# Local and downsampled attention with two expert layers: the first layer's input scale taken from v, its first two inputs split in two halves

## The chip, the cores and the metric

One core of a Trainium2 chip runs the whole program. The metric is the device time of one execution in microseconds (us), as the median of several runs. TensorE (PE) multiplies matrices, VectorE (DVE) and ScalarE (ACT) work on elements, GpSimd (POOL) helps them, and SyncE's queue (SP) issues all DMA transfers.

## What is computed

Attention over q, k, v of shape (4 batches, 8 heads, 576 tokens, 64), as the sum of a downsampled part and a part limited to a band, then two dense layers with a gate:

```python
out_d = sm_attn(q_d, k_d, v_d)              # q, k, v averaged over 4 tokens
out_up = np.repeat(out_d, factor, axis=2)
mask = np.abs(pos[:, None] - pos[None, :]) < factor
scores = np.where(mask, scale * q @ k.T, -1e9)
out_local = softmax(scores) @ v
x = (out_up + out_local)                    # to 2304 tokens x 512
h = x @ w_in;  g = h / (1 + exp(-h));        x = g @ w_out     # layer 1, 512 -> 2048 -> 512
h = x @ w_in2; g = h / (1 + exp(-1.702 * h)); out = g @ w_out2 # layer 2
```

The weights are stored as 64-bit floats. Both softmax rows are positive and sum to at most 1, so every element of x is at most twice the largest |v| of its batch.

## The kernel before

Work goes in blocks of half a batch: 8 blocks m of 288 tokens in layer 1, 9 blocks of 256 tokens in layer 2. A block of attention has four units u = 4m + hp, one for each pair hp of heads. The program is a list of named steps, each for one engine. Every engine takes its steps in the order of a table (`PLACES`, two digits for each step); tables `ON` give the engine of steps that may run on several. Before an instruction an engine waits for the semaphores of what the step depends on, and what stands behind it on that engine waits too.

**Matrix products.** Each f32 operand is held as two f16 halves, high and low, and a product is three matmuls (`TERMS`). So x must be scaled by a power of two and split: `split` makes the steps `xh` (ACT, the high half, tile xhl, L781) and `xl` (DVE, the low half, L784).

**The scale before.** When x of a unit is ready (step `XA`, DVE L1324 and L1325, tile xf), step `XM` takes the largest |x| of each partition (L1328). When all four are there, `rm` (PE, L769, two passes) sums them over the partitions by a product with ones, `am` (L773) takes the largest of four, and `pw` (three instructions in `pow2`, L286 to L288) makes the power of two and its inverse. Then `xh`, `xl`, and the first product `h1.m.0.0` (PE, L709, 12 matmuls).

**The weights at the start.** Eight loads of 1 MB for the first layer's inner weights (`ldst1in.c.j`, SP L524) and eight for the outer ones. Each is turned from 64 bits to 32 by `ca` and `cz` (ACT, L326 and L330), `cs` (DVE, L334), `sg` (ACT L347 or DVE L339) and `cp` (two half adds on DVE or POOL, L351), its scale is taken (`sps` on PE L563, `si` on DVE), and it is split by `hi` (ACT L379) and `lo` (DVE L383, tile win).

**The attention of block 0** runs beside this. For a unit: `KT` and `QT` transpose k and q on PE (tiles kps L1133, qps L1197), `KC` and `QC` copy them on ACT (QC at L1201), `SC` makes the scores (PE L1221 and L1228), `DM`, `LC`, `LS`, `LE`, `LU`, `RC`, `LN`, `DN` and `PT` are the softmax, `AV` is the product with v (PE L1310), `UC` copies a part out (ACT L1316), and `XA` makes x. Tile vw holds v's rows for the local part: all rows of a pair of heads of the batch, 768 elements in each partition.

**The loads.** The end of the kernel has a list `first` of the first loads (for each pair of heads k, q, v and a weight), but its pairs are soft: a table may put a load elsewhere. q has two buffers, so the third load of q waits until `QT0` has read the first.

Of the kernel before, what the change touches and what calls it, by code (L numbers as in the profile page):

```python
# [8 lines left out]
F32 = mybir.dt.float32  # L9
# [30 lines left out]
def on(name, usual):  # L40
# [8 lines left out]
    "0206040307050k0h0L0V00090n111u010a080J0q0U0Y180f0H0S0N0W0X1o1s0e0w0B0F0Q101C1I0K1r1v1y1z1B1R1V0T1Z1L262g2i2r2x1q2d2n2h2G2o2L2R1S2N2Z2Q"  # L49
    "3k2S3p3u1Q2y2C2O2U2W3R3X171c1e1l1O221F1P1T20252c2u2w2P2Y3x3I353a3Z4l44662m323h3c4q3L3S4w4L2K3o3H4h4r4u4H4X5Q3w4n5b4R5o5d5l5t5I3B4O505c"  # L50
    "5R5K5O616e4C5G5Z5Y64696i6v7f4z5s6a5C6C6r6I6K6Y5r6W6P7a7g7j7z7p7x65797L7i7R7n7r7W824J536f6q6z6F6b6o6H6U70766S747m7C7A7J7O7S7Y8586889u0d"
    "0i0t0O0b0c0j0o0m0v0p0r0y0z0C0A0D0M0I0R0Z12140l0u1j1p0g0s0x0E0G0P13161a1d1g1f1h1m1k1t1D1H1J191i1Y29151b1n1w1x1G1A1E1M1N281X242b2a2e2k2p"
    "2D1K232s2I1U21272j2f2v2l2t2z2A2E2B2F2H2J2M2T2V2X303334393g3b363f3C5a737e8w1W2q374t313e3i3n3q3r3s3v3y3A3E3D3J3W4042484b4D383j3z3M3G3Q3N"
    "3U41454K4f4o4y4M4Q4V4Z514e4m4p4B4v4E4G4N4W565f585g5j5q5v5B5E5M5254595i5e5m5k5p5w5A5F5D5J5L5P5S5X6062686n6D7I7P8Gci3l3t6h4k3d4i6J55678x"
    "7G6x4F8Q7N5V3Y46495n5y636j6g6p6k6G6O6Q6T757b7k6Z7K7U839z3P3T8n5T6c6t726M7E8a8d8f8h8k8l8o8r8u8B8H8L9w7v7Z8K7o7u898j8p8t8C8J8O8P8T8V9197"
    "9b9f9k9m9o8A8I9g8m8s8R928X958Z93989a9d9c9p9v9h9A9G9J9K9Pa1a7a9aqa8cd7t908U9H8E9i9L9R9T9V9Wa4aaacaeafaraxanaBaHaJb79E9Ua2adavataDaGaKaM"
# [1488 lines left out]
```

## Time and profile before

| | |
|---|---|
| median of 3 runs | 883.58 us (882.74 to 883.6) |
| the profiled execution | 883.47 us |
| its span, first to last instruction | 881.7 us |
| PE busy | 858.1 us, 97% of the span |
| DVE busy | 606.1 us, 69% |
| ACT busy | 465.1 us, 53% |
| POOL busy | 151.2 us, 17% |
| mean granted clock of TensorE | 0.986 |

The profile is of one execution. Busy time of PE is modelled for matmuls that overlap, so work on PE is counted below by starts of its instructions. A stretch is given in us from the span's start.

### The profile page before, as it was taken

The page shows a single profiled execution, that of the slowest core. Times are in us where ns is not written, and L with a number is a line of the kernel's source. Part 1 is how long each engine was busy: PE and PEld are TensorE (multiplying, and loading weights), DVE is VectorE, ACT ScalarE, POOL GpSimd, SP SyncE. Part 2 cuts the span into 40 slices and gives each one's busy share as a digit, 9 for nine tenths or more (in the row PEclk, how much of TensorE's full clock was granted, in tenths as well). Part 3 has the DMA queues.
Part 4 walks back from the last instruction along what each step waited for, and adds up shares of the span by engine and source line. Part 5 has one row for each costly group of instructions (what it writes and reads, how often), then busy time and mean ns, then how long its engine had stood idle before and what let it go on. Part 6 is the DMA issues. An engine that isn't in the chain of part 4 may idle for free.

```text
span 881.7 us, 23835 instructions
## 1 busy us (share of the span) xinstructions
PE 858.1 (97%) x10212; PEld 715.9 (81%) x10212; DVE 606.1 (69%) x1342; ACT 465.1 (53%) x824; POOL 151.2 (17%) x186
## 2 busy tenths in 40 slices
PE   6889899999999999999999999999999999999998
PEld 5777677777777777777787788888888888888887
DVE  3889999878876767576576899374474828465472
ACT  4899875645556545574643755253342525253341
POOL 1355333113212321211210011002100000020000
PEclk9869999999999999999999999999999999999999
DMA  9968666266636354533317200000000000000000
GB/s 243 288 181 244 137 116 113 45 130 147 140 66 165 105 124 94 149 94 94 121 31 280 97 1 1 25 1 1 26 26 13 13 13 2 36 2 25 1 15 35
DMA packets 114990, 75.86 MB, mean 86 GB/s; under 512 B 94788, under 2 KB 100292, under 8 KB 113860
## 3 DMA queue, kind: packets, MB, share of 16 engines
q1 hardware_dynamic: 114884, 74.34, 32.3%
q8 instruction: 80, 1.31, 0.7%
q14 instruction: 26, 0.21, 0.1%
HBM read 61.21 MB, written 13.11 MB: 84 GB/s over the span
## 4 chain that ended last, share of the span: by engine, by line
PE 85%; DVE 8%; ACT 4%; DMA 1%; issue 1%; SPq 0%; DVEq 0%; ACTq 0%
PE hps L876 20%; PE hps L709 19%; PE ops L814 19%; PE oy L955 10%; PE oz L955 5%; PE ox L955 2%; PE ul L1310 2%; PE sl L1228 2%; PE sl L1221 1%; PE ul L1304 1%; PE ops L842 1%; ACT st L326 1%; DVE wout L383 1%; DVE g L904 1%; PE tps L1287 1%
## 5 line engine op out<-in xcount | busy, mean ns | idle before, releaser
L709 PE MATMUL hps<-xhl,win 128*128 128x288 f16 x1536 | 199.3, 289 | 0.4 <-DVE tg L724 0.4
L876 PE MATMUL hps<-xhl,win 128*128 128x256 f16 x1728 | 190.3, 273 | 0.0
L876 PEld LDWEIGHTS <-win 128*128 128x128 f16 x1728 | 169.1, 98 | 19.6
L709 PEld LDWEIGHTS <-win 128*128 128x128 f16 x1536 | 148.7, 99 | 38.7 <-issue 0.5
L814 PE MATMUL ops<-g,wout 128*128 128x288 f16 x1344 | 170.9, 286 | 0.0
L955 PEld LDWEIGHTS <-g 128*128 128x128 f16 x1512 | 147.7, 98 | 19.5 <-DVE g L904 1.3
L814 PEld LDWEIGHTS <-wout 128*128 128x128 f16 x1344 | 129.8, 98 | 32.7 <-issue 0.6
L888 ACT ACTIVATE tg<-hps,blk 128x512 f32<-128x512 f32 x72 | 49.4, 687 | 127.6 <-PE hps L876 118.2
L891 DVE SCALAR_TENSOR_TENSOR tg<-tg,hps 128x512 f32<-128x512 f32 x72 | 49.2, 683 | 59.9 <-ACT tg L888 59.9
L904 DVE SCALAR_TENSOR_TENSOR g<-tg,g 128x896 f16<-128x896 f32 x72 | 77.4, 1086 | 0.6 <-ACT g L901 0.3
L955 PE MATMUL oy<-wout,g 128*128 128x256 f16 x648 | 75.1, 273 | 0.0
L901 ACT ACTIVATE g<-tg 128x896 f16<-128x896 f32 x72 | 67.4, 944 | 14.6 <-DVE tg L897 10.4
L721 ACT ACTIVATE tg<-hps,blk 128x576 f32<-128x576 f32 x64 | 47.1, 736 | 43.5 <-PE hps L709 35.7
L351 POOL TENSOR_TENSOR cs<-cs,cz 128x512 int32<-128x512 int32 x32 | 42.0, 1318 | 154.2 <-DVE cs L334 46.0
L724 DVE SCALAR_TENSOR_TENSOR tg<-tg,hps 128x576 f32<-128x576 f32 x64 | 47.8, 747 | 28.6 <-ACT tg L721 28.4
L895 POOL TENSOR_TENSOR tg<-tg 128x128 f32<-128x128 f32 x14 | 9.7, 691 | 293.6 <-DVE tg L891 264.1
L933 ACT ACTIVATE o<-oy,blk 128x256 f32<-128x256 f32 x27 | 12.7, 472 | 73.6 <-PE oy L955 73.6
L734 DVE SCALAR_TENSOR_TENSOR g<-tg,gs,g 128x576 f16<-128x576 f32 x56 | 46.8, 841 | 6.1 <-ACT g L731 6.0
L731 ACT ACTIVATE g<-tg,gs 128x576 f16<-128x576 f32 x56 | 42.6, 768 | 13.1 <-DVE tg L724 12.5
L326 ACT ACTIVATE st<-st 128x512 f32<-128x512 f32 (+1 forms) x48 | 39.6, 830 | 18.1 <-DMA st<-in_moe_w_out_dram 6.9
L939 DVE SCALAR_TENSOR_TENSOR o<-oy,blk,o 128x256 f32<-128x256 f32 x9 | 4.4, 484 | 59.0 <-PE oy L955 34.6
L351 POOL TENSOR_TENSOR x<-x,z 128x512 int32<-128x512 int32 x26 | 35.6, 1384 | 51.5 <-ACT z L330 20.7
(168 smaller groups left out, 1159.3 us busy)
## 6 DMA issues: line engine op xcount, KB each, us to landing
st<-in_moe_w_in_dram SPq DMA_DIRECT2D x8, 1024.0 KB, 9.9
st<-in_moe_w_out_dram SPq DMA_DIRECT2D x8, 1024.0 KB, 5.7
st<-in_moe_w_in_dram SPq DMA_DIRECT2D x16, 512.0 KB, 4.6
st<-in_moe_w_out_dram SPq DMA_DIRECT2D x16, 512.0 KB, 3.9
vw<-in_v_dram SPq DMA_DIRECT2D x62, 96.0 KB, 4.8
out_dram<-o SPq DMA_DIRECT2D x18, 256.0 KB, 3.3
wdin<-cs SPq DMA_DIRECT2D x16, 256.0 KB, 3.6
r<-wdin SPq DMA_DIRECT2D x4, 1024.0 KB, 4.8
```

Of the source, the lines that this page charges most:

```text
L326: ACT.activation(out=hi.bitcast(F32), in_=hi.bitcast(F32), func=AF.Copy, scale=2.0 ** -112)
L351: eng.tensor_tensor(out=s, in0=s, in1=zget()[:, o], op=ALU.add)
L709: nc.tensor.matmul(o, T[w][:, kc, a, fc * P:(fc + 1) * P], T[xk][:, kc, b, :T_], start=(n == 0), stop=(n == 3 * KC - 1))
L721: ACT.activation(out=T[tg], in_=T[ps][:, :, :T_], func=AF.Tanh, scale=T["a" + bk][:, c:c + 1])
L724: DVE.scalar_tensor_tensor(out=T[tg], in0=T[tg], scalar=1.0, in1=T[ps][:, :, :T_], op0=ALU.add, op1=ALU.mult)
L814: nc.tensor.matmul(o, w[:, j, a, dc * P:(dc + 1) * P], g[:, b, j % 2, :], start=(n == 0), stop=(n == 3 * NF - 1))
L876: nc.tensor.matmul(o, T[w][:, kc, a, fc * P:(fc + 1) * P], T[xk][:, kc, b, :], start=(n == 0), stop=(n == 3 * KC - 1))
L888: ACT.activation(out=four(), in_=T[ps][:, 0, :], func=AF.Tanh, scale=T["a" + bk][:, c:c + 1])
L891: DVE.scalar_tensor_tensor(out=four(), in0=four(), scalar=1.0, in1=T[ps][:, 0, :], op0=ALU.add, op1=ALU.mult)
L901: ACT.activation(out=T[g][:, 0], in_=T[tg], func=AF.Copy, scale=GS2)
L904: DVE.scalar_tensor_tensor(out=T[g][:, 1], in0=T[tg], scalar=GS2, in1=T[g][:, 0], op0=ALU.mult, op1=ALU.subtract)
L955: nc.tensor.matmul(T[bank[acc]], g[:, a, slot, :], w, start=first and p == p0 and i == 0, stop=prod in (2, 3, 4) and p == NF // 2 - 1 and ...
```

## The change

It has four parts. (1) In layer 1 the scale of x comes from v. `VM`, one for each batch and pair of heads, takes the largest |v| of each partition of tile vw (768 elements); `XM` is gone. `dx` takes the largest of the four and puts it on the diagonal of a 128 x 128 tile, `rm` multiplies this by ones (f32, 128 columns), and `am` takes the largest of 128. Both blocks of a batch share the scale (`scale_of`), so `dx`, `rm`, `am`, `pw` and the step that scales the gate run for the even blocks alone. (2) `split` makes x of blocks 0 and 1 in two halves, `xh..a`, `xl..a` for the first two pairs of heads and `xh..b`, `xl..b` for the others; the product `h1.m.0.0` waits for both. (3) The tables `ON` and `PLACES` are new. (4) The pools of layer 1 are released after `VM`, `XA` and `am`, where it was `XM`. The list `first` is the same.

```diff
@@ split
-        bank = ("pa1", "rm" + bk, 4 * n + 3.9) if L.n == 1 else ("pr", "rm" + bk)
+        sk = scale_of(L, n)
+        bank = ("pa1", "rm" + bk, 4 * n + 2.9) if L.n == 1 else ("pr", "rm" + bk)
+
+        def z():
+            DVE.tensor_reduce(out=small(L, n, 7), in_=mget(), axis=AX.X, op=ALU.max)
+            T["dg" + bk] = pools["at"].tile([P, 1, P], F32, tag="dg", name="dg", bufs=1)[:, 0]
+            DVE.tensor_scalar(out=T["dg" + bk], in0=T["ident"], scalar1=small(L, n, 7), scalar2=None, op0=ALU.mult)
 
         def a():
...
-            nc.tensor.matmul(T["rm" + bk][:, :KC], ones32, mget(), start=True, stop=True)
+            if L.n == 1:
+                nc.tensor.matmul(T["rm" + bk][:, :P], ones32, T["dg" + bk], start=True, stop=True)
+            else:
+                nc.tensor.matmul(T["rm" + bk][:, :KC], ones32, mget(), start=True, stop=True)
...
-            pow2(T["am" + bk], 1, 13, T["inv" + bk], T["s" + bk], t)
+            pow2(T["am" + bk], 1, 13 - 8 if L.n == 1 else 13, T["inv" + bk], T["s" + bk], t)
+
+        parts = ((0, 2), (2, KC)) if L.n == 1 and n < 2 else ((0, KC),)
 
-        def hi():
-            T[xk] = pools["xhl" + ln].tile([P, KC, 2, T_], F16, tag="xhl", name="xhl")
-            ACT.activation(out=T[xk][:, :, 0, :], in_=src(), func=AF.Copy, scale=T["s" + bk])
+        def hi(k0, k1):
+            if k0 == 0:
+                T[xk] = pools["xhl" + ln].tile([P, KC, 2, T_], F16, tag="xhl", name="xhl")
+            ACT.activation(out=T[xk][:, k0:k1, 0, :], in_=src()[:, k0:k1], func=AF.Copy, scale=T["s" + sk])
...
@@ unit
-        def xmax():
-            DVE.tensor_reduce(out=small(L1, m, 10 + hp), in_=T[X][:, hp, :], axis=AX.X, op=ALU.max, apply_absolute_value=True)
-
+        if half == 0:
+            def vmax():
+                DVE.tensor_reduce(out=small(L1, m, 10 + hp), in_=T[vw].rearrange("p e d -> p (e d)"), axis=AX.X, op=ALU.max,
+                                  apply_absolute_value=True)
+            add("VM" + nm, "DVE", dve(4 * NBL * D), vmax, r=[vw], w=[("vm", b, hp)])
```

Of the tables the diff shows only other digits, so three places of the program follow as they stand on the engines. A DMA that stands on SP in one row with "x2" is two transfers.

DVE from `XA3` to the last part of x of block 0 (tile xf is x, xhl its split, win the inner weights, wi and ibin their scale, x_80 the weights on their way). Before:

```order
L1324 TENSOR_TENSOR xf<-ul_793,us 128x3x24
L1325 TENSOR_TENSOR xf<-ul_794,us 128x2x3x24
L1328 TENSOR_REDUCE blk<-xf 128x1
L383 SCALAR_TENSOR_TENSOR win_2_825<-x_80,bin_88,win_2_825 128x2x512
L773 TENSOR_REDUCE blk<-rm 128x1
L286 TENSOR_SCALAR blk<-blk 128x1
L287 TENSOR_SCALAR blk<-blk 128x1
L288 RECIPROCAL blk<-blk 128x1
L443 TENSOR_REDUCE wi_101<-sps 128x1
L748 TENSOR_SCALAR blk<-ibin_87,blk 128x1
```

and after nine more instructions for the weights' scale and a conversion comes `xl`, L784. Now:

```order
L285 TENSOR_SCALAR blk<-blk 128x1
L286 TENSOR_SCALAR blk<-blk 128x1
L287 RECIPROCAL blk<-blk 128x1
L350 ISA x_80<-x_80,z 128x1024
L333 TENSOR_SCALAR x_80<-st_617 128x1024
L1350 TENSOR_TENSOR xf<-ul_812,us 128x3x24
L1350 TENSOR_TENSOR xf<-ul_813,us 128x3x24
L1351 TENSOR_TENSOR xf<-ul_814,us 128x2x3x24
L801 SCALAR_TENSOR_TENSOR xhl<-xf,blk,xhl 128x2x288
L382 SCALAR_TENSOR_TENSOR win_2_787<-x_80,bin_88,win_2_787 128x2x512
L801 SCALAR_TENSOR_TENSOR xhl<-xf,blk,xhl 128x2x288
```

The scale (L285 to L287) stands ahead of `XA3`, and between `XA3` and the last part of x are only the first half and one `lo`.

DVE further ahead, where the maxima of v stand (tile pd and sc are the softmax, nm and mx its maxima; dg is the diagonal). Now:

```order
L382 SCALAR_TENSOR_TENSOR win_1_614<-x_80,bin_88,win_1_614 128x2x512
L333 TENSOR_SCALAR x_80<-st_558 128x1024
L1355 TENSOR_REDUCE blk<-vw 128x1
L1262 TENSOR_REDUCE nm<-sl 72x2
L1269 TENSOR_TENSOR sc<-sl,cap 128x192
L1272 TENSOR_REDUCE mx<-sc 128x6
L442 TENSOR_REDUCE wi_101<-sps 128x1
L774 TENSOR_REDUCE blk<-blk 128x1
L776 TENSOR_SCALAR dg<-ident,blk 128x128
L1350 TENSOR_TENSOR xf<-ul_701,us 128x3x24
```

This is the last of four `VM` (L1355) and `dx` (L774, L776), ahead of `XA2`.

SP at the first loads, from v of the first pair of heads on (st is a weight, vw is v). Before:

```order
L1099 DMA vw<-in_v_dram 28x64
L524 DMA st_223<-in_moe_w_in_dram 128x2x1024
L524 DMA st_225<-in_moe_w_in_dram 128x2x1024
L1053 DMA qraw<-in_q_dram 96x3x64 x2
L1053 DMA kraw<-in_k_dram 96x6x64 x2
L1099 DMA vw<-in_v_dram 32x12x64 x4
```

Now:

```order
L1125 DMA vw<-in_v_dram 28x64
L1079 DMA qraw<-in_q_dram 96x3x64 x2
L523 DMA st_253<-in_moe_w_in_dram 128x2x1024
L523 DMA st_255<-in_moe_w_in_dram 128x2x1024
L1079 DMA kraw<-in_k_dram 96x6x64 x2
L1125 DMA vw<-in_v_dram 32x12x64 x4
```

The third load of q moved ahead of the second and third weight. The first two loads changed places as well: k before q, and PE begins with `KT0.0`, then `QT0`.

## Rows read from the trace of the kernel before

**Rows 1.** Stretches: us, then busy us (instructions) by engine, PE clock, DMA.

```profile
31.60:52.90 21.30, 15.45 (x310) 13.77 (x304) 18.38 (x45) 21.27 (x38) 9.88 (x9) 0.79 0.91 256
52.90:59.10 6.20, 6.20 (x82) 5.55 (x81) 5.89 (x19) 6.20 (x9) 1.02 (x1) 0.50 0.46 150
59.10:134.50 75.40, 70.74 (x1146) 54.62 (x1135) 72.55 (x174) 62.38 (x110) 33.87 (x30) 0.97 0.70 165
134.50:881.70 747.20, 742.56 (x8384) 621.54 (x8380) 494.77 (x1063) 357.48 (x637) 99.82 (x116) 1.00 0.24 66
```

**Rows 2.** Timeline, PE up to the first product: start us, us, instruction.

```profile
52.84 1.87 PE L563 MATMUL sps<-x,ones 128*128 128x128 bf16 x16 [0.66 <-DVE x L334]
...
54.89 2.89 PE L1197 MATMUL qps<-four,qraw 96*128 96x120 f32 x12
57.76 0.76 PE L1221 MATMUL sl<-kd,qT 64*72 64x144 f32 x4
...
59.14 2.52 PE L709 MATMUL hps<-xhl,win 128*128 128x288 f16 x12
```

**Rows 3.** Timeline of ACT, the same stretch.

```profile
52.54 0.43 ACT L1316 ACTIVATE us<-ul 128x288 f32<-128x288 f32 x1
...
56.08 1.28 ACT L781 ACTIVATE xhl<-xf,blk 128x1152 f16<-128x1152 f32 x1
57.23 0.48 ACT L1201 COPY qT<-qps 128x360 f32<-128x360 f32 x1
```

**Rows 4.** Timeline of DVE, the same stretch.

```profile
53.01 0.37 DVE L1324 TENSOR_TENSOR xf<-ul,us 128x72 f32<-128x72 f32 x2 [0.22 <-ACT us L1316]
53.29 0.30 DVE L1325 TENSOR_TENSOR xf<-ul,us 128x144 f32<-128x144 f32 x1
...
54.00 1.27 DVE L383 SCALAR_TENSOR_TENSOR win<-x,bin,win 128x1024 f16<-128x1024 f32 x1
55.19 0.15 DVE L773 TENSOR_REDUCE blk<-rm 128x1 f32<-128x4 f32 x1
...
55.76 0.17 DVE L288 RECIPROCAL blk<-blk 128x1 f32<-128x1 f32 x1
...
57.43 1.41 DVE L784 SCALAR_TENSOR_TENSOR xhl<-xf,blk,xhl 128x1152 f16<-128x1152 f32 x1
```

**Rows 5.** Groups by line and shape, DVE, 0 to 140 us: busy us, mean ns.

```profile
L724 DVE SCALAR_TENSOR_TENSOR tg<-tg,hps 128x576 f32<-128x576 f32 x9 | 6.6, 738 | 0.8 <-ACT tg L721 0.7
...
L351 DVE CUSTOM_DVE_ANT_0 x<-x,z 128x1024 uint16<-128x1024 uint16 x6 | 4.7, 787 | 0.0
L339 DVE TENSOR_SCALAR z<-st 128x1024 uint16<-128x1024 uint16 x6 | 4.4, 740 | 0.0
...
L1328 DVE TENSOR_REDUCE blk<-xf 128x1 f32<-128x288 f32 x8 | 3.6, 449 | 0.2
...
L1148 DVE TENSOR_REDUCE kd<-kT 128x144 f32<-128x576 f32 x4 | 2.9, 729 | 0.0
L784 DVE SCALAR_TENSOR_TENSOR xhl<-xf,blk,xhl 128x1152 f16<-128x1152 f32 x2 | 2.8, 1414 | 0.0
```

**Rows 6.** Groups by line and shape, DVE, whole span.

```profile
L1480 DVE TENSOR_REDUCE blk<-x 128x4 f32<-128x1024 f32 x9 | 10.9, 1211 | 0.0
```

**Rows 7.** Groups by line and shape, PE, whole span.

```profile
L769 PE MATMUL rm<-blk,ones 128*128 128x4 f32 x34 | 5.6, 234 | 0.0
...
L427 PE MATMUL sp<-dg,ones 128*128 128x128 f32 x8 | 1.5, 274 | 0.0
```

**Rows 8.** Timeline of SP's queue, 9 to 12 us.

```profile
9.62 0.91 SPq L524 DMA_DIRECT2D st<-in_moe_w_in_dram  x2
10.72 0.85 SPq L1053 DMA_DIRECT2D qraw<-in_q_dram  x2
```

**Rows 9.** Timeline of PE, its first two steps.

```profile
6.80 1.61 PE L1197 MATMUL qps<-four,qraw 96*128 96x120 f32 x6 [6.80 <-DMA qraw<-in_q_dram]
8.40 2.89 PE L1133 MATMUL kps<-four,kraw 96*128 96x120 f32 x12
```

More of the change, by code (lines that the diff above doesn't have):

```diff
@@ L720, in tanh @@
             T[tg] = pools["tg" + ln].tile([P, 2, T_], F32, tag="tg", name="tg")
-            ACT.activation(out=T[tg], in_=T[ps][:, :, :T_], func=AF.Tanh, scale=T["a" + bk][:, c:c + 1])
+            ACT.activation(out=T[tg], in_=T[ps][:, :, :T_], func=AF.Tanh, scale=T["a" + sk][:, c:c + 1])
         def g0():
@@ L741, in h_pair, with scale_of @@
         plan.users[g].append(plan.steps[-1])
+    def scale_of(L, n):
+        return f"{L.n}.{n - n % 2 if L.n == 1 else n}"
     def a_scale(L, n, cs):
@@ L785, in lo @@
+        parts = ((0, 2), (2, KC)) if L.n == 1 and n < 2 else ((0, KC),)
[3 more added lines that the diff above has]
+            ACT.activation(out=T[xk][:, k0:k1, 0, :], in_=src()[:, k0:k1], func=AF.Copy, scale=T["s" + sk])
+        def lo(k0, k1):
+            DVE.scalar_tensor_tensor(out=T[xk][:, k0:k1, 1, :], in0=src()[:, k0:k1], scalar=T["s" + sk], in1=T[xk][:, k0:k1, 0, :],
                                      op0=ALU.mult, op1=ALU.subtract)
@@ L787, in split @@
         sc2 = ["scope2"] if L.n == 2 else []
-        add("rm" + bk, "PE", 0.2, a, r=mkey + sc2, w=["rm" + bk], alloc=[bank])
-        add("am" + bk, "DVE", 0.16, b, r=["rm" + bk], w=["am" + bk])
-        add("pw" + bk, "DVE", 0.5, d, r=["am" + bk], w=[("inv", bk)])
-        add("xh" + bk, "ACT", act(KC * T_, 1), hi, r=skeys + [("inv", bk)] + sc2, w=[(xk, "h"), xk], alloc=[("xhl" + ln, xk)])
-        add("xl" + bk, "DVE", dve(KC * T_), lo, r=skeys + [("inv", bk), (xk, "h"), xk], w=[(xk, "l")], lock=True)
+        if L.n == 1 and n % 2 == 0:
+            add("dx" + bk, "DVE", 0.45, z, r=mkey, w=["dg" + bk], alloc=[("dg", "dg" + bk)])
+            mkey = ["dg" + bk]
@@ new lines, in split @@
+        if L.n == 2 or n % 2 == 0:
+            add("rm" + bk, "PE", 0.2, a, r=mkey + sc2, w=["rm" + bk], alloc=[bank])
+            add("am" + bk, "DVE", 0.16 if L.n == 2 else 0.28, b, r=["rm" + bk], w=["am" + bk])
+            add("pw" + bk, "DVE", 0.5, d, r=["am" + bk], w=[("inv", bk)])
+        for k0, k1 in parts:
+            e = "" if k1 == KC else "0"
+            tag = bk + ("" if len(parts) == 1 else "ab"[k0 > 0])
+            x = skeys if L.n == 2 else skeys[k0:k1]
+            add("xh" + tag, "ACT", act((k1 - k0) * T_, 1), lambda k0=k0, k1=k1: hi(k0, k1), r=x + [("inv", sk)] + sc2 + ([xk] if k0 else []),
+                w=[(xk, "h" + e)] + ([] if k0 else [xk]), alloc=[] if k0 else [("xhl" + ln, xk)])
+            add("xl" + tag, "DVE", dve((k1 - k0) * T_), lambda k0=k0, k1=k1: lo(k0, k1), r=x + [("inv", sk), (xk, "h" + e), xk], w=[(xk, "l" + e)], lock=True)
@@ L1359, in unit @@
         uses_x.setdefault(m, []).append(s)
-        add(f"XM{u}", "DVE", dve(HALF), xmax, r=[(X, hp)], w=[(X, hp, "m")])
-        plan.users[X].append(plan.steps[-1])
-        plan.steps[-1].keys.add(X)
     uses_x = {}
@@ L1407 @@
         split(L1, m, lambda m=m: T[f"xf{m}"], [(f"xf{m}", hp) for hp in range(NHP)],
-              [(f"xf{m}", hp, "m") for hp in range(NHP)], lambda m=m: small(L1, m, 10, KC), HALF, None)
+              [("vm", m // 2, hp) for hp in range(NHP)], lambda m=m: small(L1, m, 10, KC), HALF, None)
         for s in plan.steps[i0:]:
-            if s.name[:2] in ("xh", "xl", "rm"):
+            if s.name[:2] in ("xh", "xl"):
                 plan.users[f"xf{m}"].append(s)
@@ L1415 @@
                 a_scale(L1, m, [c])
-        else:
+        elif half == 0:
             a_scale(L1, m, list(range(NC)))
@@ L1455, in scope2 @@
         pools["xhl2"] = es2.enter_context(tc.tile_pool(name="xhl2", bufs=2, reuse_waits="tile"))
-    att = [s for s in plan.steps if s.name[:2] in ("XM", "wd", "as", "LN", "so", "si", "pw") or s.name.startswith("xl1")]
+    att = [s for s in plan.steps if s.name[:2] in ("VM", "XA", "am", "wd", "as", "LN", "so", "si", "pw") or s.name.startswith("xl1")]
     add("scope2", "NONE", 0.0, scope2, w=["scope2"], after=att)
```

93 lines of the change are left out of this document (46 added, 47 removed), and 21 rows, old and new, of the table ON.

## The prediction

> **What bounds the kernel now.** I read the page first: PE is busy for 97% of the span, so the question is where the rest lies. The busy times by stretch answer it [rows 1]. From 134.5 us to the end PE is busy for 742.56 of 747.2 us: nothing that feeds it matters there unless it runs dry, and DVE has 252 us to spare. From 59.1 to 134.5 us two engines are nearly full at once, DVE with 72.55 and PE with 70.74 of 75.4 us: DVE still converts weights and makes the gate's halves, PE does the first block's products. Ahead of that, from 31.6 to 52.9 us, ACT is full (21.27 of 21.3), DVE has 2.9 us left, and PE is not the bound. So the time can move in two ways: the first product at 59.14 us may start sooner, and DVE may be sooner with its list up to 134.5 us. Then I read the timelines of three engines from `UC3` (ACT, 52.54) to this product [rows 2 to 4], and the groups by line for prices [rows 5 to 7].
>
> The reader is to see a tail of 6.60 us between `UC3` and the first product. DVE makes `XA3` from 53.01 to 53.59, then the maximum of x, one `lo`, the scale from 55.19 to 55.93, seven small steps and a conversion, and ends `xl` at about 58.76 [rows 4]. ACT can start `xh` only at 56.08 [rows 3]. [...]
>
> **The sum, part by part.**
>
> The tail. With the scale ready before `XA3`, I lay the new order out by the old prices, from the start of `UC3`. `XA3` ends at +1.05 (53.59). ACT makes the first half of `xh` behind `UC3`, a weight step of 1.05, and the second half: half of 1152 elements is 576, on DVE 0.738 against 1.414 for the whole [rows 5], so a half is 0.74; on ACT I take half of 1.28 and the same 0.06 more, 0.70. The second half ends near +2.9. DVE goes on from +1.05 with 0.74, a `lo` of 1.2 (1.27 less overlap) and 0.74 and has all of x at +3.7, where it was +6.22: **2.5 us sooner**. PE transposes q from +1.05, 2.87 us at the lower clock, and makes scores for 1.38: the first product at +5.3, where it was +6.60: 1.3 us sooner. It is PE, not x, that would then be last.
>
> What is put in front of the tail. Ahead of `XA3` DVE gets four `VM`. No row has 768 elements; 576 take 0.729 and 1024 take 1.211 [rows 5, 6], which bound one, and I take 0.93 on the line between them: 3.7. `dx` is two short instructions, at most the 0.449 of a 288-element maximum each [rows 5] and at least nothing; I take 0.4. `am` and `pw` move here, 0.74 [rows 4], 0.1 more for the longer `am`. Three `XM` of 0.449 leave: -1.35. By the tables two more `sg` of 0.65 (0.740 less overlap) and one more `cp` of about 0.65 (0.787 with two double ones among six) stand here [rows 5]: 1.9. Together **5.4 us more work** ahead of `XA3`. About 2.2 of it stands in the first 31.6 us, where DVE waits for transfers and PE for more than half of the time, and I cost that part at nothing; if this cover were gone it would be 2.2. The other 3.2 meet the 2.9 us that DVE has idle from 31.6 to 52.9 [rows 1]. If they fill every gap, `XA3` slips by 0.3; if they fill none, by 3.2. The gaps are many and short and a maximum of v waits only for a load, so it fills well: I take **1.0 us later**, near the lower end.
>
> The first loads. The load of q for unit 2 now stands ahead of two weights on SP, and it waits for `QT0`, which stands behind `KT0.0`. Before, the weights went out at 9.62 and q at 10.72 [rows 8]. With k first, `KT0.0` takes 2.7 and `QT0` 1.6 from 6.80 on [rows 9]: q goes out at 11.1 and the weights at 12.0, 2.4 us later. Behind them wait every later load of SP and, on ACT and DVE, the conversions. Lower bound nothing, since the DMA engines are at work on what was issued before; upper bound 2.4 for all that follows. The scores of unit 0 come no later than before, and by 31 us ACT has the same amount of steps behind it in both orders, so I take 0 and keep 2.4 for the range.
>
> From the tail to 134.5 us. The same steps remain for DVE: 142 from `xl` to the first gate of block 1 before, 139 now. `XM4` to `XM7` are gone (4 x 0.449), block 1's own `am` and `pw` too (0.74), and three `VM` of batch 1 moved in (2.8) with two halves (0.06): even. As DVE is the fuller of the two, the end of this stretch follows DVE: 2.5 less 1.0 is **1.5 us sooner**. PE has 4.7 us idle there and takes this up.
>
> PE's own work. `rm` is two matmuls, and 8 of layer 1 become 4. By starts a pair cost about 0.25 at full clock, and a pair with 128 columns is near it (means of 234 and 274 [rows 7]). Three of the four that are saved stand after 134.5 us: **0.6 us less**, by busy time at most 1.4, at least nothing.
>
> After 134.5 us DVE loses and gains the same (per batch 8 x 0.449 against 4 x 0.93), beside 252 idle us; a new table may bring PE a wait or take one away. PE has 4.6 us idle in that stretch, part of it at its very end; I take 0, between a gain of 1 and a loss of 3.
>
> Sum: -1.5 - 0.6 = -2.1 from the profiled 883.47: 881.4. The median of the runs is 0.11 above the profiled run, which changes nothing here: **881.4 us**.
>
> [...] In the rows two halves of 576 cost 2 x 0.738 where the whole is 1.414, so a cut costs 0.06 us on DVE [rows 5]. [...]
>
> **The rivals.**
>
> (A) The forecast: the tail shortens and DVE carries v's maxima in its gaps.
>
> (B) DVE has no room. `XA3` slips by 2.5, in the upper part of 0.3 to 3.2, and eats the tail: -2.5 + 2.5 - 0.6 gives 882.9. For it: DVE is busy for 18.38 of 21.3 us already. Against it: all but one of the `VM` may run long before they are needed.
>
> (C) Slower: the load of q blocks SP. Weights 2.4 us late, and `XA3` late by this and by the 3.2 that then find no gap, since DVE waits for weights in order: -2.5 + 2.4 + 3.2 - 0.6 is +2.5, 886.0. It decides from a slip of `XA3` of 4.9 us on (2.5 + 0.6 + 1.8). For it: a `cs` of the delayed weight stands on DVE ahead of unit 1's scores. Against it: transfers overlap.
>
> (D) A larger gain: PE also loses waits in 59.1 to 134.5, where it idles for 4.7 us, because DVE's list is better placed: 3 us more, 878.4.
>
> That the change does not do what it says: the product waits for both halves, so the halves only let two engines overlap; but the order on DVE shows the scale ahead of `XA3`, so the tail must change. No chance of its own.
>
> **How the numbers follow.** A measurement of this kernel can tell about 0.2%, 1.8 us: faster is below 881.8, slower above 885.4. A has 0.42, of which 0.27 lie below 881.8 and 0.15 above; B has 0.22, with 0.20 within 0.2% and 0.02 slower; C has 0.21, slower; D has 0.15, faster. Faster 0.42, same 0.35, slower 0.23. The range reaches from D's place, 878, to 1 us beyond C's, 887, and leaves out some 0.2, where a new table does worse or better than any of these.
>
> **What would show it.** Right: the first product at 57 to 59 us, `XA3` at 53.5 to 55, all of x about 2.6 us behind it; DVE at 95% or more from 20 us on; the end of the dense stretch 1 to 3 us sooner. Wrong: `XA3` after 57 us (B or C); ACT or DVE waiting for a weight's transfer between 15 and 25 us (C); PE idle by more than 6 us after 134.5, which would be a cause that I cost at nothing.

## The result, and the profile after

The changed kernel is slower: 889.12 us median of 4 runs (886.41 to 890.47) against 883.59 beside it, ratio 1.0064 with a 95% interval of 1.0040 to 1.0087. Run again unedited it gave 889.39 (886.61 to 891.43), ratio 1.0068 (1.0049 to 1.0087). The forecast of 881.4 had the wrong sign, and the time lies above the range.

The loss arises before 140 us. Two profiles of the changed kernel, one of 886.41 us and one of 891.43, called the quick and the slow one below, show how it is spread. The first product of block 0 starts at 61.91 and 64.22 us (59.14 before), that of block 1 at 138.0 and 142.2 (134.5 before); from there to the end it is 746.6 and 747.5 us (747.2 before). For the quick one this sums to 2.8 + 0.7 - 0.6 = 2.9 us, the difference of the spans (884.6 and 881.7); for the slow one to 5.1 + 2.6 + 0.3 = 8.0.

The busy times by stretch of the quick profile (us, then PE, weight loads, DVE, ACT, POOL with instructions, PE's clock, DMA share, GB/s):

```profile
31.60:57.60 26.00, 18.06 (x352) 16.05 (x326) 24.64 (x54) 22.38 (x40) 15.00 (x10) 0.74 0.92 260
57.60:61.90 4.30, 4.25 (x72) 3.61 (x71) 4.11 (x8) 4.30 (x7) 1.14 (x1) 0.60 0.94 249
61.90:138.00 76.10, 70.47 (x1139) 53.89 (x1132) 74.41 (x173) 61.95 (x114) 34.37 (x29) 0.98 0.61 153
138.00:884.60 746.60, 742.14 (x8382) 621.30 (x8374) 493.41 (x1038) 357.62 (x639) 107.77 (x117) 1.00 0.24 65
```

Beside [rows 1]: up to `XA3` it is DVE that is now full (24.64 of 26.0 us, where it was 18.38 of 21.3), and ACT has idle time. The last stretch is as it was.

The tail itself does what the change says. DVE of the quick profile (start, duration), which answers to [rows 4]:

```profile
57.71 0.37 DVE L1350 TENSOR_TENSOR xf<-ul,us 128x72 f32<-128x72 f32 x2
58.00 0.30 DVE L1351 TENSOR_TENSOR xf<-ul,us 128x144 f32<-128x144 f32 x1
58.38 0.98 DVE L801 SCALAR_TENSOR_TENSOR xhl<-xf,blk,xhl 128x576 f16<-128x576 f32 x1
59.28 1.27 DVE L382 SCALAR_TENSOR_TENSOR win<-x,bin,win 128x1024 f16<-128x1024 f32 x1
60.47 0.81 DVE L801 SCALAR_TENSOR_TENSOR xhl<-xf,blk,xhl 128x576 f16<-128x576 f32 x1
```

From the start of `XA3` to all of x it is 3.57 us (57.71 to 61.28), before 5.83. But `XA3` starts 4.7 us later. PE of the same profile, as [rows 2]:

```profile
58.11 2.50 PE L1223 MATMUL qps<-four,qraw 96*128 96x120 f32 x12
60.54 0.76 PE L1247 MATMUL sl<-kd,qT 64*72 64x144 f32 x4
61.23 0.76 PE L1254 MATMUL sl<-kT,qT 64*32 64x32 f32 x48
61.91 3.06 PE L709 MATMUL hps<-xhl,win 128*128 128x288 f16 x12
```

Where do 4.7 us come from? First the sum over all that stands ahead of `XA3`, before and in the quick profile, with the two groups of DVE that grew by their length (residues `lo`, then bit steps `cs`; busy us, mean ns):

```profile
0.00:53.01 53.01, 38.67 (x619) 34.32 (x619) 32.94 (x90) 39.12 (x71) 16.55 (x40) 0.88 1.02 256
L383 DVE SCALAR_TENSOR_TENSOR win<-x,bin,win 128x1024 f16<-128x1024 f32 x4 | 5.7, 1456 | 0.6 <-ACT win L379 0.6
L334 DVE TENSOR_SCALAR x<-st 128x1024 int32<-128x1024 int32 x8 | 5.7, 727 | 0.6 <-ACT st L326 0.6
```

```profile
0.00:57.71 57.71, 40.53 (x627) 36.34 (x628) 39.78 (x99) 39.06 (x71) 21.30 (x41) 0.85 0.95 253
L382 DVE SCALAR_TENSOR_TENSOR win<-x,bin,win 128x1024 f16<-128x1024 f32 x4 | 6.9, 1743 | 0.1
L333 DVE TENSOR_SCALAR x<-st 128x1024 int32<-128x1024 int32 x8 | 7.3, 921 | 0.9 <-ACT st L325 0.9
```

DVE is busy for 6.8 us more (39.78 for 32.94) and idle for 2.1 less (17.93 for 20.07): the difference is the slip. Of the 6.8, some 2.7 are the same twelve residues and bit steps, only longer. In time, `UC2` (ACT) starts at 46.81, 1.3 later than before (45.55). Unit 3 then takes 10.5 us to `UC3` at 57.30, before 7.0 (52.54). DVE and PE of the quick profile there:

```profile
43.07 3.48 DVE L382 SCALAR_TENSOR_TENSOR win<-x,bin,win 128x1024 f16<-128x1024 f32 x2
46.48 1.75 DVE L333 TENSOR_SCALAR x<-st 128x1024 int32<-128x1024 int32 x1
48.15 0.94 DVE L1355 TENSOR_REDUCE blk<-vw 128x1 f32<-128x768 f32 x1
49.01 0.44 DVE L1262 TENSOR_REDUCE nm<-sl 72x2 f32<-72x288 f32 x1
```

```profile
45.08 0.71 PE L1336 MATMUL ul<-PT,vw 32*64 32x24 f32 x48
48.28 1.01 PE L562 MATMUL sps<-x,ones 128*128 128x128 bf16 x8 [2.49 <-DVE x L333]
51.03 0.79 PE L781 MATMUL rm<-dg,ones 128*128 128x128 f32 x2 [1.74 <-DVE xf L1350]
51.62 2.77 PE L1198 MATMUL vps<-vw,vsum 128*72 128x128 f32 x12
```

Unit 3's scores were ready at 44.5 us (`SC3` on PE), and DVE took them at 49.01, behind two residues, a bit step and the last maximum of v. PE waited for the bit step, then for x of unit 2 ahead of `rm`, and v's transposes stood behind. POOL's additions ran beside DVE's first two rows (43.31, 4.37 us for two), and these took longer than alone: 3.48 for two of 1.27, 1.75 for one of 0.68.

### The profile page after: what moved, and what is told of

Its sections match the earlier page's. It is cut to its first block, busy times and chain, and to the rows that moved or that the text cites. A ratio compares the mean times of both kernels' runs of the same rounds, so it can differ in the third digit from the quotient of the medians.

```text
span 884.6 us, 23807 instructions
## 1 busy us (share of the span) xinstructions
PE 857.3 (97%) x10204; PEld 715.1 (81%) x10204; DVE 611.7 (69%) x1315; ACT 462.8 (52%) x828; POOL 164.5 (19%) x187
## 4 chain that ended last, share of the span: by engine, by line
PE 86%; DVE 7%; DMA 2%; SPq 1%; ACT 1%; issue 1%; POOL 1%; DVEq 0%; ACTq 0%
PE hps L709 20%; PE hps L902 20%; PE ops L840 19%; PE oy L981 11%; PE oz L981 5%; PE ox L981 3%; PE ul L1336 2%; DMA vw<-in_v_dram 2%; PE sl L1254 2%; DVE wout L382 1%; PE ops L868 1%; PE sl L1247 1%; PE ul L1330 1%; PE tps L1313 1%; DMA kraw<-in_k_dram 1%
## 5 line engine op out<-in xcount | busy, mean ns | idle before, releaser
L721 ACT ACTIVATE tg<-hps,blk 128x576 f32<-128x576 f32 x64 | 47.1, 737 | 24.7 <-PE hps L709 21.3
L350 POOL TENSOR_TENSOR x<-x,z 128x512 int32<-128x512 int32 x25 | 39.9, 1610 | 27.0 <-ACT z L346 9.3
```

Source lines behind the costliest of these rows:

```text
L350: eng.tensor_tensor(out=s, in0=s, in1=zget()[:, o], op=ALU.add)
L721: ACT.activation(out=T[tg], in_=T[ps][:, :, :T_], func=AF.Tanh, scale=T["a" + sk][:, c:c + 1])
```

## The experiments

Theories at the start: more work on DVE (maxima of v, diagonal); the new table (order, engines); the first loads; and, once seen, a toss (which of two engines starts first) that makes the runs differ. Step names are those of the text above; `lk`, `lqqraw`, `vw` are the loads of k, q, v. Each time is a median of 4 to 12 runs, beside 9 to 23 of the kernel before (882.7 to 883.3). Where only places move, the diff shows the order on an engine.

**1. The changed kernel again.** No edit.

> The changed kernel once more, unedited. Its five-run times lay between 886.4 and 890.5 us while the kernel before stays within 1 us. Theory 'noise of one chip': this time it stays within 1 us, near 886 to 889. Theory 'its order sits on an edge' (some transfer or wait that falls one way or the other): it spreads over 3 us or more again, and the spans differ by as much. The profile should again show XA3 near 57.7 us and the first product of block 0 near 61.9, against 53.0 and 59.1 before.

889.39 (886.61 to 891.43): it spreads over 5 us again. The profile taken was of the longest run; on DVE it is the same as the quick one to 0.02 us up to 24.2 us. POOL and DVE of the quick profile, then of the slow one:

```profile
24.76 1.82 POOL L350 TENSOR_TENSOR x<-x,z 128x512 int32<-128x512 int32 x1 [6.91 <-ACT st L325]
```

```profile
24.76 0.69 DVE L333 TENSOR_SCALAR x<-st 128x1024 int32<-128x1024 int32 x1 [0.21 <-ACT st L325]
```

```profile
24.69 1.27 POOL L350 TENSOR_TENSOR x<-x,z 128x512 int32<-128x512 int32 x1 [6.83 <-PE sps L562]
```

```profile
24.77 1.75 DVE L333 TENSOR_SCALAR x<-st 128x1024 int32<-128x1024 int32 x1 [0.22 <-ACT st L325]
```

In the slow profile POOL starts 0.08 us ahead of DVE, keeps its own length, and DVE takes 1.06 us longer; in the quick one both start at 24.76, DVE keeps its 0.69 us, and POOL takes 0.55 us longer. In the slow profile, where DVE lost, PE waited for its result, and what followed on PE ran at a granted clock of 0.50 (27 to 31 us):

```profile
26.57 1.01 PE L562 MATMUL sps<-x,ones 128*128 128x128 bf16 x8 [0.77 <-DVE x L333]
27.38 1.57 PE L1223 MATMUL qps<-four,qraw 96*128 96x120 f32 x6
28.75 2.77 PE L1159 MATMUL kps<-four,kraw 96*128 96x120 f32 x12
```

Those 12 transposes take 1.50 us in the quick profile. The stretches say the same, quick first:

```profile
27.00:31.00 4.00, 4.00 (x36) 3.71 (x34) 3.90 (x10) 3.27 (x6) 0.30 (x1) 0.90 1.08 372
```

```profile
27.00:31.00 4.00, 4.00 (x23) 4.00 (x21) 3.83 (x13) 1.84 (x3) 0.51 (x1) 0.50 1.06 386
```

From 34 us on every ACT step of the slow profile is 2.7 to 3.0 us behind the quick one: 1.1 from the toss, the rest from the clock. That the lost toss brings the low clock is not shown: in the profiles of the kernels 2, 9, 10 and 17 DVE loses the same toss, and the granted clock is 1.00 from 24 to 34 us. Kernel 10, its PE wait (1.26 us, longer than the 0.77) and its stretch:

```profile
26.25 0.62 PE L562 MATMUL sps<-x,ones 128*128 128x128 bf16 x8 [1.26 <-DVE x L333]
24.00:34.00 10.00, 7.54 (x166) 6.59 (x166) 9.62 (x23) 8.69 (x14) 3.77 (x3) 1.00 1.15 275
```

Those four are no faster in the median (888.36, 889.70, 888.63 and 891.64).

**2. The first steps as before.**

```diff
 SP
-lk0.0 lqqraw0 lk0.1 lqqraw1 vw0.0 lqqraw2 ldst1in.0.2 ldst1in.1.0
+lqqraw0 lk0.0 lqqraw1 lk0.1 vw0.0 ldst1in.0.2 ldst1in.1.0 lqqraw2
 ACT
-KC0.0 QC0 DE0 LE0 ca1.in.0.0 KC0.1 QC1 cz1.in.0.0
+cz1.in.0.0 ca1.in.0.0 QC0 KC0.0 DE0 LE0 QC1 KC0.1
 PE
-KT0.0 QT0
+QT0 KT0.0
```

> The changed kernel, with only the first steps put back: q ahead of k in the first two loads, q of unit 2 behind two more weights on SP, the first weight's two ACT conversions at the head of ACT, q's transposes ahead of k's. Theory 'first loads': the weights go out 3 us sooner (near 9.7 us in place of 12.7), ACT starts near 6 in place of 10.5 us, and XA3 comes 2 to 4 us sooner, near 54 to 56; time 3 us less than the changed kernel's, 884 to 886. Theories 'more work on DVE' and 'order of unit 3': XA3 moves by under 1 us and the time by under 1 us.

888.36, ratio 1.0057 (1.0041 to 1.0073), 0.8 to 1.0 less than the changed kernel and within its interval. The weights do go out 3 us sooner, SP of the changed kernel and of this one:

```profile
12.69 0.97 SPq L523 DMA_DIRECT2D st<-in_moe_w_in_dram  x2
```

```profile
9.68 0.91 SPq L523 DMA_DIRECT2D st<-in_moe_w_in_dram  x2
```

but `XA3` starts at 57.07, only 0.6 sooner: the load was covered, and this theory falls.

**3. Small maxima of v.** Of v's 768 elements 64 are looked at; the rest of the maximum is left out.

```diff
-in_=T[vw].rearrange("p e d -> p (e d)"), axis=AX.X, op=ALU.max,
+in_=T[vw][:, 1, :], axis=AX.X, op=ALU.max,
```

> The changed kernel, with each maximum of v taken over 64 of its 768 elements (the rest of v's maximum is left out, all else is kept). 0.91 to 0.94 us of DVE a piece become some 0.2, so about 2.9 us of DVE work ahead of XA3 go and 5.8 up to the end of the stretch. Theory 'more work on DVE': XA3 and the first product come 2.5 to 3 us sooner, time 3 to 4 us less. Theory 'first loads' or 'order of unit 3': DVE only waits longer, XA3 moves by under 1 us, time by under 1.5 us.

887.44, ratio 1.0049 (1.0031 to 1.0066): 1.7 to 1.9 less for 2.9 us of work ahead of `XA3` (197 ns each in place of some 930), but the interval overlaps that of the unedited kernel. In its profile, of the longest run (889.73), `XA3` starts at 60.17, where the slow profile of the unedited kernel has 60.53: seen there, smaller maxima bring next to nothing.

**4 to 8. Repairs of the order**, each made to the changed kernel.

```diff
 4 PE
-sps1.in.1.0 QT2
+QT2 sps1.in.1.0
 5 ON
-cp1.in.0.0a on POOL
+cp1.in.0.0a on DVE, ahead of cp1.in.0.0b
 6 DVE
-lo1.in.0.2 lo1.in.1.2 cs1.in.2.2 VM0.3 DM3 LC3
+DM3 LC3 lo1.in.0.2 lo1.in.1.2 cs1.in.2.2 VM0.3
 7 DVE
-lo1.in.0.2 lo1.in.1.2 cs1.in.2.2 VM0.3 DM3 LC3 si1.2 dx1.0 XA2
+VM0.3 dx1.0 lo1.in.0.2 lo1.in.1.2 cs1.in.2.2 DM3 LC3 XA2 si1.2
 8 DVE
-lo1.in.0.2 lo1.in.1.2 cs1.in.2.2 VM0.3 DM3 LC3 si1.2 dx1.0 XA2 LU3 RC3 si1.2p am1.0 DN3
+VM0.3 dx1.0 DM3 LC3 cs1.in.2.2 XA2 lo1.in.0.2 LU3 RC3 am1.0 DN3 si1.2
...
```

> The changed kernel with one step of PE moved: the transposes of q for unit 2 go ahead of the third sum of a weight's bits (the one that waits 0.77 us for DVE in the slow profile and not at all in the quick one). Theory 'PE's clock': in the slow profile of the changed kernel that gap kept the granted clock at 0.50 from 25 to 34 us, k's and v's transposes took 2.77 in place of 1.50 us, and all that follows is 2.8 us late; with the gap filled the clock is at 1.0 from 28 us on in every run, so the runs lie within about 1 us, near 886.5, and the median is 2 to 3 us less. [...]

> The changed kernel with GpSimd's first addition for a weight (1.27 us alone) given to DVE (0.67 us). In the profiles it begins within 0.07 us of a DVE instruction and either it takes 1.82 us or that DVE instruction takes 1.75 in place of 0.69. Theory 'toss of DVE against GpSimd, then PE's clock': no toss is left, the spread falls to about 1 us, the median is 1.5 to 3 us less. Rival 'DVE is full': 0.67 us more of DVE work comes through, the median is as before or 0.7 us more.

> The changed kernel with unit 3's first two softmax steps on DVE put ahead of two weight residues, a bit step and the last maximum of v (four instructions that took 6.6 us there in the quick profile). Theory 'order of unit 3': its scores were ready at 44.5 us and DVE took them at 49.0; now at about 42.5 to 45, XA3 comes 2 to 4 us sooner, time 2 to 4 us less. Rival 'DVE is full': the same work stands ahead of XA3 and it comes within 1 us of where it was; time within 1 us.

> The changed kernel with the scale's own chain moved forward: the last maximum of v and the diagonal ahead of two residues on DVE, unit 2's x right behind its last ACT step, and so the product that spreads the maximum (rm) 3 us sooner on PE. Theory 'rm on PE': rm must stand ahead of v's transposes of unit 3 on PE, since it takes the PSUM bank between units 2 and 3, and there PE waited 2.49 and 1.74 us in the quick profile, then worked at half clock; now it waits for the third bit sum alone, XA3 comes 1.5 to 3 us sooner and the time falls by 1.5 to 3 us from 889, to 886 to 887.5. Rival 'DVE is full whatever its order': within 0.7 us of 889.

> The changed kernel with unit 3's whole passage laid out anew (58 steps from unit 2's turn of its weights to unit 3's copy): maximum of v and diagonal first, then unit 3's softmax, unit 2's x, the third bit sum, rm, v's transposes, unit 3's weights; the two residues behind. Theory 'order around unit 3 and rm': XA3 near 54 to 55.5 us in place of 57.7, time 884 to 886. Rival 'DVE is full': XA3 within 1 us of 57.7 and the time within 1 us of 888.

In this order 890.44, 887.57, 888.24, 889.12 and 889.27. Only the second is faster by more than 1 us (the first is as much slower): without that addition on POOL the ratio is 1.0052 (1.0039 to 1.0065), which overlaps the changed kernel's interval, and the runs lie within 2.4 us. In 4 the moved transposes themselves waited 1.46 us, for DVE's x of unit 0, so no gap was filled: the clock stayed at 0.50 from 26 to 35 us, and the theory of the clock was not tested by it. In 6 `DM3` starts at 44.79 in place of 49.01, and `UC3` comes at 57.69 all the same: PE then waits 3.39 us for the bit step, and the softmax's division stands behind `am`, which waits for `rm`. In 8 `UC3` comes 1.2 sooner (56.15), but `XA3` ends at 58.6, no sooner (58.3): a bit step stands ahead of it on DVE and takes 1.75 us, beside two additions on POOL (54.63 to 57.58).

```profile
56.38 1.75 DVE L333 TENSOR_SCALAR x<-st 128x1024 int32<-128x1024 int32 x1
```

So no single place holds the loss.

**9, 10. Combinations.** 2, 4 and 6 together, and 2 with 8.

> The changed kernel with three things at once: first steps as before, unit 3's softmax ahead of four fillers on DVE, q of unit 2 ahead of the third bit sum on PE. If the losses add up (first steps 1, order of unit 3 2 to 3, clock 2 to 3), the time is 882 to 884 and XA3 near 54 us. If they are all the same loss (DVE is full whatever its order), 886 to 887.

> As the kernel with unit 3's passage laid out anew, and the first steps as before too (q ahead of k, weights ahead of unit 2's q, two conversions at the head of ACT). If the first steps count once unit 3's order is out of the way, 882 to 884.5 and XA3 near 53; if they still do not, the same as without them within 0.7 us.

889.70 and 888.63: the losses do not add up. The five runs of 10 lie within 0.4 us (888.57 to 888.98): here the spread is gone and the loss is not.

**11. The maxima of v in the kernel before**, results unread.

```diff
 DVE of before
+VM0.0 behind PT0, VM0.1 behind DN1, VM0.2 behind lo1.in.1.0, VM0.3 behind XA2
```

> The kernel before, with four maxima of v added on DVE ahead of XA3 (behind unit 0's turn, behind unit 1's division, behind a residue, behind unit 2's x), whose results nobody reads; nothing else is changed. 4 x 0.93 = 3.7 us of DVE work more. Theory 'more work on DVE' in full: XA3 3 to 3.7 us later, time 886 to 887. My sum's term (they lie in gaps, 1 us comes through): 884 to 885. Rival 'the order is what costs': under 0.5 us, 883 to 884.

885.49, ratio 1.0026 (1.0017 to 1.0035): 2.3 us for 3.7 us of work, by the median. The profile is of the quickest run (883.65); in it `XA3` starts at 54.16 and the first product at 60.30, each 1.2 later than before. Its ten runs spread from 883.65 to 886.73, where the kernel before stays within 1.6 us beside it. The first maximum stands at 22.28 us, ahead of two bit steps that PE waits for.

**12. The same with the first maximum moved** behind those bit steps and a conversion (`sg1.in.1.0`), where DVE of the kernel before idled for 1.18 us.

> The kernel before with the four added maxima of v (results unread), as in the earlier run, but the first one stands behind the first bit steps of unit 1's weights, where DVE idled for 1.18 us at 24.5 us, in place of ahead of two bit steps that PE waits for at 22 to 24 us. Theory 'PE's clock is set at 22 to 27 us': with the bit sums undelayed the clock returns to 1.0 at 27 us in every run, the spread of 3 us goes, and the median falls from 885.5 to 883.5 to 884.5. Rival 'work alone': 885.5 again, with the same spread.

884.11, ratio 1.0020 (1.0010 to 1.0030): 1.4 us. Only two of twelve runs are above 885.4, but these are at 887.2, so the spread has not gone. The 0.9 us less than in 11 is not shown: the intervals overlap.

**13 to 16. Computation and table apart.** Old computation in the new table; new computation in the old table, twice (the first time the later maxima of v stood too early); and the new scale for block 0 alone in the old table (13 in the order old computation, 14 and 15 new computation, 16 block 0).

> The computation of the kernel before (maxima of x, one scale for each block, x whole) in the changed kernel's table and engine assignment, as far as its steps are the same; maxima of x stand behind each unit's x, a block's product, maximum and scale some six PE steps behind its last unit. Theory 'the table': the new table alone costs most of the 5.9 us, so this stays at 886 to 889, with XA3 at 56 to 58 us. Theory 'the computation' (maxima of v on DVE, and rm ahead of unit 3's transposes): without them XA3 is near 54 to 55 and the time 883 to 885.

> The new computation (maximum of v, halves of x, half of the scales) laid into the table and the engine assignment of the kernel before: the four maxima of v stand on DVE where the maxima of x stood or next to them, the first loads and unit 3's softmax as before. Theory 'more work on DVE' (maxima of v, the diagonal and the scale ahead of XA3, 2.8 us of work more): XA3 slips by 1 to 3 us and the time stays above 884. Theory 'the new table' (order of first loads, order on DVE and ACT, which engine gets what): XA3 stays within 1.5 us of the 53.0 before, x is ready 2 us sooner behind it, and the time is 881.5 to 883.5.

> The whole new computation in the table and assignment of the kernel before, once more: this time the maxima of v of the later batches stand behind the second unit of their batch, where v has landed (in the first try DVE waited 6.2 us for v's load at 99 us, and later ones the same). Theory 'the table': 883 to 886, as in block 0 alone. Theory 'the computation': 887 or more. If waits behind 140 us come back (PE waiting over 3 us there), it tells of my placing and not of either.

> The kernel before, with the change in block 0 alone: four maxima of v in place of four of x, the diagonal and the wider product, x in two halves; the table of before otherwise, rm between v's and the softmax's transposes of unit 3. Compared with the kernel that only had the four maxima added (885.5), 1.8 us of maxima of x leave, 0.6 for the diagonal comes, and the scale leaves the tail. Theory 'the table': 883 to 885, with x ready 2 us sooner behind UC3 and XA3 at 54 to 55.5. Theory 'the computation': 886 or more, as rm holds up unit 3 in any table.

Whole times: 902.23, 914.25, 904.73 and 886.16 (ratio of the last 1.0036, 1.0023 to 1.0048). The first three carry waits of PE that my placing made, most of them behind 140 us (in the first try at the old table DVE waited 6.21 us for a load of v at 99 us, and PE 6.65 at 101), so the expected totals fail. Only the profiles up to block 1's first product tell something, and of 14 not even these. Ahead of `XA3` (start at the end of the stretch; DVE's busy time is the third), new computation in the old table (15), then old computation in the new table (13) with its residues and bit steps:

```profile
0.00:55.86 55.86, 39.16 (x622) 35.02 (x623) 35.09 (x97) 39.16 (x71) 17.27 (x40) 0.86 0.98 243
0.00:55.97 55.97, 40.61 (x627) 36.75 (x628) 36.85 (x92) 38.87 (x71) 19.49 (x41) 0.84 0.99 259
L382 DVE SCALAR_TENSOR_TENSOR win<-x,bin,win 128x1024 f16<-128x1024 f32 x4 | 6.9, 1742 | 0.1
L333 DVE TENSOR_SCALAR x<-st 128x1024 int32<-128x1024 int32 x8 | 6.8, 861 | 1.9 <-ACT st L325 1.8
```

The new computation alone puts 2.2 us more on DVE (35.09 for 32.94) and `XA3` comes 2.9 later; the new table alone, without any maximum of v, puts 3.9 more on it (36.85) and `XA3` comes 3.0 later, with residues as long as in the changed kernel. From the first product of block 0 to that of block 1:

| | table before | table after |
|---|---|---|
| old computation | 59.14 to 134.5: 75.4 us | 61.95 to 139.7: 77.8 us |
| new computation | 62.16 to 134.3: 72.1 us | 61.91 to 138.0: 76.1 us |

In either table the new computation saves time here (3.2 and 1.7 us), and with either computation the new table costs (2.4 and 4.0). These are single profiles: the slow one of the changed kernel takes 77.9, where the 1.7 is gone. Nor are the cells alike in all else: in the old table the maxima of batch 1 stand behind this stretch (from 135.3 us), and the old computation in the new table has two waits of PE of 1.8 and 1.9 us that come from my placing of its steps or from the table. Ahead of the first product each costs some 3 us alone, and both together not more, in the quick profile. What the new table does in this stretch shows in one group of rows. The residues of the outer weights (busy us, mean ns), before; the changed kernel; old computation in the new table; new computation in the old table:

```profile
L383 DVE SCALAR_TENSOR_TENSOR wout<-x,bout,wout 128x1024 f16<-128x1024 f32 x8 | 10.1, 1276 | 0.0
```

```profile
L382 DVE SCALAR_TENSOR_TENSOR wout<-x,bout,wout 128x1024 f16<-128x1024 f32 x8 | 13.7, 1744 | 0.0
```

```profile
L382 DVE SCALAR_TENSOR_TENSOR wout<-x,bout,wout 128x1024 f16<-128x1024 f32 x8 | 12.3, 1562 | 0.0
```

```profile
L383 DVE SCALAR_TENSOR_TENSOR wout<-x,bout,wout 128x1024 f16<-128x1024 f32 x8 | 10.1, 1273 | 0.0
```

The same eight instructions take 3.7 us longer in the changed kernel (8 x 0.47). With the old computation the new table makes 2.3 of it (8 x 0.29). In the profiles with the old table the mean is 1272 to 1277 throughout, in those with the new computation in the new table 1668 to 1749. Where they are long POOL works beside them: two that begin at 119.83 take 4.02, while POOL converts v from 119.83 to 122.76. In the old table they run clear of it.

**17. The maxima of batch 1 later**: the three that stand at 134 to 138 us in the changed kernel go behind block 1's first product.

> The changed kernel with the three maxima of v of the second batch that stand on DVE ahead of block 1's first product moved behind it (0.91 to 0.95 us each, beginning at 134.0, 135.3 and 137.9 us; the first two end ahead of 138.0). Between the first product of block 0 and that of block 1 the changed kernel takes 76.1 us, the kernel before 75.4, the new computation in the table of before 72.1 to 72.7. Theory 'DVE's list counts to its end': 1.9 us less in this stretch, time 1.5 to 2 us less than 889. Theory 'it is lost earlier, at 62 to 127 us' (PE waits for nothing from 126.8 us on in the profile, and DVE instructions lengthened beside GpSimd make 6.7 us there against 4.4): no change, within 0.7 us.

891.64, ratio 1.0096 (1.0080 to 1.0111): 2.3 to 2.5 us slower, which neither theory expected. The stretch takes 77.9 us in its profile, as in the slow profile of the unedited kernel, with the same wait in it (`SC` 1.74 us at 65.6; 1.76 at 67.6), and behind it `rm` waits 1.0 at 157. So the end of DVE's list in this stretch gains nothing; where the further 2 us went is open.

**18. What the runs point to.** New scale for the first two blocks only, x of block 0 in halves, the table and engines of before, and the maxima of v in free places:

```diff
 DVE of before, without XM0 to XM7, am1.1, pw1.1
+VM0.0 behind sg1.in.1.0, VM0.1 behind XA1, VM0.2 behind LN2, VM0.3 behind lo1.in.1.2
+dx1.0 behind XA2, am1.0 behind DN3, xl1.0a behind XA3
 PE of before
-AV3 sps1.in.3.0 sps1.in.3.2 rm1.0
+rm1.0 TP3 AV3 sps1.in.3.0 sps1.in.3.2
```

> The new computation for the first two blocks only (one scale from the first batch's v, x of block 0 in two halves; maxima of x and scales of the other blocks as before), in the table of before, with the maxima of v in the places that the traces left free: the first in the 1.18 us gap at 24.5 us, the others where the maxima of x stood. If the tail's 2 us and the 2.5 us of maxima and scales that leave block 1 come through and the clock stays: 880.5 to 882.5, faster than both. If the maxima of v still push PE into its lower clock: 884 to 886.

882.03 (11 runs, 880.30 to 883.08) against 882.69, ratio 0.9986 (0.9978 to 0.9995): faster than both kernels, by a little. Its stretches:

```profile
61.31:134.00 72.69, 69.53 (x1139) 54.03 (x1134) 70.49 (x164) 62.37 (x110) 35.37 (x30) 0.98 0.69 172
134.00:880.60 746.60, 742.52 (x8382) 621.55 (x8380) 493.55 (x1062) 357.50 (x637) 99.89 (x116) 1.00 0.25 66
```

and DVE at the first maximum, whose place is the gap of before:

```profile
24.43 0.94 DVE L1356 TENSOR_REDUCE blk<-vw 128x1 f32<-128x768 f32 x1
```

The first product is 2.2 us late (61.31), the stretch behind it 2.7 us shorter with 164 DVE instructions for 174, the rest 0.6 shorter: together 1.1 less span. Kernel 16 has the same computation in block 0 and other places for it, and took 886.16; by the stretches some 2 of these 4 us are block 1's maxima and scale, which 18 does without, and that leaves some 2 to the places.

## Why the prediction was wrong, step by step

**"`XA3` slips by 1.0, near the lower end of 0.3 to 3.2": the step that failed.** It slipped by 4.7 in the quick profile, 7.5 in the slow one. The prices were right or near: a maximum of v took 0.91 to 0.95 (0.93 taken), `dx` 0.59 (0.4). Two terms around them were wrong.

The first is the work. I counted 5.4 us more ahead of `XA3`, 1.9 of it by the new table (two `sg`, one `cp`). It was 6.8, and the table alone, with the old computation, put 3.9 on DVE: besides the added steps, its residues and bit steps had become longer (1742 ns for 1456 and 861 for 727; in the changed kernel 1743 and 921). I had priced only the steps that were added, and put what the table does to the others at nothing.

The second is the cover. I let 4.4 of the 5.4 us vanish in gaps, 2.2 of them in the first 31.6 us. DVE's idle time fell by 2.1 in all, and in the first 31.6 us DVE did only 0.6 more (15.13 for 14.56). For maxima whose results nobody reads the forecast was near: 1.2 us at `XA3` in the quickest run of kernel 11, though its median lost 2.3. With the scale hanging on them, in the same table, `XA3` came 2.9 later for 2.2 us of work, and DVE idled more than before (20.77 for 20.07): there the work did not fill gaps. These are one profile each.

**"The same steps remain: even", from the tail to block 1.** I counted DVE's work and left out its length. Without the maxima of x (and with those of batch 1 moved out) it was 72.1 us for 75.4 in the old table, and the new table took it back: residues 0.47 us longer each, eight times. The count of steps cannot show this; no row of before did either, since there these residues ran at 1276.

**What I did not have at all** is the toss at 24.8 us and PE's clock behind it, some 2.8 us between two profiles of one program. Its share of the median is not measured: taking away the addition on POOL gave 1.5 to 1.8 us within overlapping intervals, and that profile shows the clock at 0.50 from 26 to 32 us too. The low clock from 24 to 34 us is hardly what the median loses: kernel 10, whose five runs lie within 0.4 us and whose profile has none of it, took 888.63. How the 5.5 to 6.2 us divide between DVE's longer instructions, the order around unit 3 and the clock behind 34 us stays open.

**The tail** was right: 2.3 us sooner for all of x (2.5 predicted, from an end of `xl` at 58.76 that was 58.84), and from `UC3` to the first product 4.6 (5.3). For q's transposes the sum has the 2.87 us of before, at a granted clock of 0.50 [rows 1, 2]; in the quick profile they took 2.43 (58.11 to 60.54), where the stretch has 0.60. PE, as predicted, was last behind it. In the profiles of the kernels 3, 7 and 8 the gain from `UC3` on is gone (6.7 to 7.0 us): `XA3` itself starts 1.6 to 1.9 us behind `UC3` there (0.4 in the quick profile), behind a bit step of 1.75.

**First loads, 0 with a bound of 2.4**: 0.8 to 1.0 measured, not told from none. Weights were 3.1 late (2.4 predicted). **From 134.5 on, 0.6 less**: 746.6 for 747.2 in the quick profile, the predicted size. But the slow one has 747.5, and kernel 18 has 746.6 too with nearly all the products `rm` of before, so the saved products are not shown to be its cause.

**The rivals.** C had the sign and nearly the place (a slip of 4.9 us decides; 4.7 came in the quick profile; its 886.0 is near that run's 886.41 and 3 us under the median), but half its mechanism, the blocked SP, fell in experiment 2; its other half, DVE's work that finds no gap, is in part what the runs show. B's premise, DVE without room, held from 31.6 us on (1.4 us idle in 26.0, where it was 2.9 in 21.3), at a smaller price than the true one.

**The halves.** Three of four took 0.80 to 0.81 (the fourth, 0.98, began beside an addition on POOL), so a cut of 1.414 into two costs 0.2 us on DVE. On ACT two halves of 0.76 in place of 1.28 cost 0.24. Taken from rows was 0.06 each.

## What to carry to other kernels

Where a table fixes the order, judge an edit and its new table apart: put the new computation into the old table, step by step, before believing either. Do not count on an engine's idle time to take up new work (in kernel 15 2.2 us more on DVE made `XA3` 2.9 us later, and DVE idled for 20.77 us where it was 20.07); look at whether the work stands in the gap itself, what is queued behind it and who waits for that. On DVE, count durations that may lengthen beside GpSimd (0.69 us became 1.75 here), not only instructions.

## What the runs showed of the hardware

In the two profiles of the changed kernel a bit step of DVE and an addition of POOL start within 0.08 us of each other (24.69 to 24.77 us); one keeps its length, the other takes longer. DVE's bit step of 0.69 us took 1.75 beside POOL's addition of 1.27 in the slow profile, and POOL's addition took 1.82 beside DVE's 0.69 in the quick one.

New to me was what hangs on it. Which of the two took longer differed between two profiles of one program, and 1.1 us there had become 2.8 us at 34 us: behind the lost toss PE ran at a granted clock of 0.50 from 25 to 34 us, in the quick profile only up to 28. The toss does not settle the clock, though. Behind waits of PE of 1.26 to 1.32 us for the same bit step it stayed at 1.00 in the kernels 2, 10 and 17.
